# Expert rows are multiplied by their gate as they leave PSUM, and the gather adds a token's row into the token's tile

## The chip, the cores and the metric

The kernel runs on one NeuronCore of a Trainium2 chip. Its compute engines are TensorE (PE; matmuls, with the loads of their stationary operand listed apart as PEld), VectorE (DVE), ScalarE (ACT) and GpSimd (POOL); SyncE (SP) issues most of the DMA transfers. Each engine works through its own queue in order, and semaphores tie the queues together. Matmul results lie in PSUM, everything else on the core in SBUF. The metric is the time of one execution in microseconds; lower is better. Times given for the kernel are medians of several runs, while the rows of the profile come from one profiled execution.

## The reference

Three parts follow one another. Attention runs over 4 batches of 576 positions with 8 heads of 64 (pooled and banded attention, added), which gives 2304 token rows of 512 numbers. A mixture of experts updates them, and a SwiGLU layer follows. What matters here is the second part:

```python
skip_score = x @ w_skip                   # x: 2304 x 512
do_compute = skip_score > 0
xc = x[do_compute]
logits = xc @ w_gate                      # 8 experts
e_idx = np.argmax(logits, axis=1)
gate_w = softmax(logits)[np.arange(len(xc)), e_idx]
for e in range(E):
    mask = e_idx == e
    h = np.maximum(xc[mask] @ w1[e], 0.0)      # 512 -> 1024
    y[mask] = gate_w[mask, None] * (h @ w2[e]) # 1024 -> 512
out[do_compute] = xc + y
```

and the third: `g = x @ w_gate; val = x @ w_val; out = (silu(g) * val) @ w_out` with 1536 hidden units. So each token that takes part gets its expert's row times one number, its gate, and that is added to the token's own row.

## The kernel before, in words

The 2304 tokens are 18 tiles of 128 (NTILE); tile i lies in SBUF as xr[i], 128 partitions of 512 float32 numbers. Every expert has 192 slots (CAP). The kernel has three stages.

**Planned stage (0 to about 193 us).** Attention, and for groups of two or three tiles the routing: logits by TensorE, then a chain of small VectorE operations that gives every token a slot number, idx (line 796), and its gate, gw (line 805). GpSimd then scatters the tile's rows, split in two float16 halves (xhl), to their slots in a DRAM buffer xs by an indirect DMA (g_x, line 858). The order of all this is not written by hand. A class Plan takes a list of operations, each with an engine, a cost, what it needs and a priority, lists them by simulated time, and emits them in that order; where it sees TensorE waiting, it puts filler matmuls on zeros (fill, line 411). After the stage's first 14 tiles, xa (line 824) loads expert 0's rows transposed; the last 4 tiles (NOH) reach expert 0 by one-hot matmuls (line 845) instead, which write into the same PSUM banks xb, and scatter their rows a little later.

**Experts (193 to 337 us).** This order is written by hand, in a loop over e from 0 to 7. SP loads weights through six staging tiles stg (lines 361, 364), ACT and VectorE split each into two float16 halves (w, lines 340 and 343); h (hp, line 1060 for expert 0 and line 1048 for the others), yb (the last 64 slots, line 1079) and ya (the first 128, line 1084) are matmuls. The output leaves PSUM times 2^-8, a fixed scale of the split, by VectorE (y_put_short, line 1088) and ACT (y_put_long, line 340), and SP writes it to a DRAM buffer ys (lines 1091, 1097). Staging is a closed loop: a new load is issued when a conversion frees its tile. For tiles 0 to 2 the rows of the last expert come by matmuls with a selection matrix (sel_y, sel_p, lines 1117 to 1132), so that they need not pass through DRAM.

**SwiGLU (337 us to the end).** While its first gv steps run, the later tiles are fetched: GpSimd gathers each token's row from ys into a tile yg (xp_g, line 1202), and VectorE multiplies it by the token's gate and adds the token's row (xp_1, line 1210):

```python
dve.scalar_tensor_tensor(out=t if i > 2 else xr[i], in0=t, scalar=gw[:, i:i + 1],
                         in1=xr[i], op0=ALU.mult, op1=ALU.add)
```

Then the tile is split (xphl) and transposed by SP's DMA. A gather is issued three tiles ahead. Each gv step is 12 matmuls into two PSUM tiles; ACT (sg, line 1262), VectorE (sg, line 1267), ACT (u) and GpSimd (u, line 346) turn the result into the next operand. At the same time conv_next turns one half-tile after another of the SwiGLU weights into float16 pairs: ACT (lines 1156, 1157), VectorE (stg, line 1163, and cb, line 1164), ACT and GpSimd (w, line 346).

## Time and profile before

| | us |
|---|---|
| median of 3 runs | 780.03 (777.61 to 780.44) |
| the profiled execution | 783.18 |
| its span | 781.0 |
| PE busy | 731.2 (94%) |
| DVE busy | 387.4 (50%) |
| ACT busy | 337.0 (43%) |
| POOL busy | 235.1 (30%) |
| line 1210 on DVE, tiles 3 to 17 (15 adds) | 31.9 |

The busy shares are averages over three stages with different limits: DVE is at 50% over the span, though in the stretch from 345 to 465 us it has hardly a gap, and after that hardly any work. So what a change is worth is read from the stretch it touches, and each stretch is listed apart in the section of rows below.

### The profile page before, as it was taken

Reading aid. Unit: us, or ns where it says so; the run is one execution under the profiler, and the core shown is the slowest. Engines: PE = TensorE matmul, PEld = TensorE weight load, DVE = VectorE, ACT = ScalarE, POOL = GpSimd, SP = SyncE. Lnnn points to the kernel's source line nnn. Section 1 sums busy time; section 2 is a strip of 40 time slices with the busy share of each in tenths; the row PEclk is TensorE's granted clock in tenths of the full one; section 3 lists DMA queues with packets and bytes.
Section 4 is the critical chain, followed back from the end, with each engine's and each line's share of the span. In section 5 each row is a group of like instructions: output and inputs, shape, how many; then the busy total and the mean of one; then the engine's idle time right before and its main releaser. Section 6 shows DMA issues by size and latency. Waiting matters only on the chain.

```text
span 781.0 us, 16260 instructions
## 1 busy us (share of the span) xinstructions
PE 731.2 (94%) x6699; PEld 485.5 (62%) x6699; DVE 387.4 (50%) x740; ACT 337.0 (43%) x650; POOL 235.1 (30%) x217
## 2 busy tenths in 40 slices
PE   9997879899799989979998789999999999999998
PEld 6776767778688867856665444466456546655653
DVE  6684687786678877769998980011001101100110
ACT  5673555442567756737667660122112202211210
POOL 5346565444000000437667660022002201210210
PEclk9998889999999999999999999999999999999999
DMA  8889878452999999845677711100000000000001
GB/s 271 243 267 243 190 197 194 137 132 86 310 309 344 315 306 303 279 151 186 168 192 197 177 28 40 41 14 1 14 28 1 1 27 14 1 14 28 1 0 41
DMA packets 88803, 107.23 MB, mean 137 GB/s; under 512 B 44720, under 2 KB 62130, under 8 KB 88151
## 3 DMA queue, kind: packets, MB, share of 16 engines
q1 hardware_dynamic: 84791, 98.23, 44.1%
q0 software_dynamic: 2880, 6.89, 2.9%
q8 instruction: 53, 0.87, 0.5%
q10 hardware_dynamic: 1056, 1.05, 0.4%
q14 instruction: 23, 0.19, 0.1%
HBM read 81.69 MB, written 17.30 MB: 127 GB/s over the span
## 4 chain that ended last, share of the span: by engine, by line
PE 41%; DVE 11%; issue 2%; ACT 2%; POOL 1%; DVEq 0%; ACTq 0%
PE gvp L1254 23%; PE op L1284 17%; DVE yg L1210 4%; DVE stg L1163 2%; DVE cb L1164 2%; DVE sg L1267 1%; DVE xphl L346 1%; ACT stg L1156 1%; POOL w L346 0%; DVE xpT L346 0%; ACT stg L1157 0%; PE xpp L1218 0%; ACT u L340 0%; ACT xpT L340 0%; ACT sg L1262 0%
## 5 line engine op out<-in xcount | busy, mean ns | idle before, releaser
L1254 PE MATMUL gvp<-xpT,w 128*128 128x384 f16 (+1 forms) x1776 | 283.8, 322 | 7.8 <-ACT sg L1262 3.6
L1254 PEld LDWEIGHTS <-w 128*128 128x128 f16 x1776 | 170.9, 98 | 119.9 <-issue 9.8
L1267 DVE SCALAR_TENSOR_TENSOR sg<-sg,gvp 128x384 f32<-128x384 f32 x72 | 39.6, 550 | 227.2 <-PE gvp L1254 222.6
L346 POOL TENSOR_TENSOR u<-sg,u 128x384 f16<-128x384 f32 x72 | 67.3, 935 | 256.8 <-ACT u L340 256.5
L1284 PE MATMUL op<-w,u 128*128 128x512 f16 x648 | 141.0, 379 | 3.3 <-ACT sg L1262 1.8
L1284 PEld LDWEIGHTS <-u 128*128 128x128 f16 x648 | 63.4, 98 | 79.6 <-issue 4.0
L343 DVE SCALAR_TENSOR_TENSOR w<-stg,w 128x1024 f16<-128x1024 f32 x64 | 77.8, 1244 | 17.6 <-ACT w L340 17.5
L340 ACT ACTIVATE u<-sg 128x384 f16<-128x384 f32 x72 | 37.5, 521 | 109.4 <-DVE sg L1267 109.3
L346 POOL TENSOR_TENSOR w<-cb,w 128x512 f16<-128x512 f32 x36 | 49.8, 1383 | 99.1 <-ACT w L340 97.8
L340 ACT ACTIVATE w<-stg 128x1024 f16<-128x1024 f32 x64 | 65.3, 1050 | 12.5 <-DMA stg<-in_moe_w 11.6
L340 ACT ACTIVATE y<-op 128x512 f32<-128x512 f32 x18 | 10.7, 596 | 117.6 <-PE op L1284 117.6
L1048 PEld LDWEIGHTS <-w 128*128 128x128 f16 x672 | 57.1, 100 | 4.9 <-issue 3.3
L1048 PE MATMUL hp<-xe,w 128*128 128x192 f16 x672 | 58.2, 250 | 0.0
L1262 ACT ACTIVATE sg<-gvp 128x384 f32<-128x384 f32 x72 | 35.0, 486 | 38.5 <-PE gvp L1254 37.6
L1084 PE MATMUL ya<-w,hT 128*128 128x512 f16 (+1 forms) x216 | 42.9, 356 | 0.0
L1164 DVE SCALAR_TENSOR_TENSOR cb<-stg 128x512 int32<-128x512 int32 x36 | 40.9, 1135 | 3.4
L511 PE MATMUL qkd<-qks,identh 128*128 128x192 f16 x192 | 34.8, 350 | 0.0
L340 ACT ACTIVATE w<-cb 128x512 f16<-128x512 f32 x36 | 22.7, 630 | 26.8 <-DVE cb L1164 26.7
L411 PE MATMUL wbank<-wz 128*128 128x252 bf16 x209 | 31.3, 290 | 2.3 <-POOL wz L407 1.3
L1084 PEld LDWEIGHTS <-hT 128*128 128x128 f16 x216 | 20.5, 98 | 20.3 <-issue 1.6
L1210 DVE SCALAR_TENSOR_TENSOR yg<-yg,gw,x 128x512 f32<-128x512 f32 x15 | 31.9, 2135 | 0.0
L539 POOL TENSOR_TENSOR vr<-vr 72x1024 f32<-72x1024 f32 x8 | 19.0, 2372 | 39.5 <-DMA vr<-in_vr 39.5
(146 smaller groups left out, 877.5 us busy)
## 6 DMA issues: line engine op xcount, KB each, us to landing
stg<-in_moe_w SPq DMA_DIRECT2D x64, 512.0 KB
qk<-in_qk SPq DMA_DIRECT2D x24, 384.0 KB
stg<-in_moe_w_out SPq DMA_DIRECT2D x12, 512.0 KB
stg<-in_moe_w_gate SPq DMA_DIRECT2D x11, 512.0 KB
stg<-in_moe_w_val SPq DMA_DIRECT2D x11, 512.0 KB
vw<-in_vw SPq DMA_DIRECT2D x18, 284.4 KB
vr<-in_vr SPq DMA_DIRECT2D x8, 576.0 KB
up<-outd SPq DMA_DIRECT2D x18, 256.0 KB
```

Of the source, the lines that this page charges most:

```text
L340: act.activation(out=o, in_=i, func=func, scale=s)
L343: dve.scalar_tensor_tensor(out=o, in0=i, scalar=s, in1=h, op0=op, op1=ALU.subtract)
L346: eng.tensor_tensor(out=o, in0=i, in1=h, op=ALU.subtract)
L511: pe.matmul(out=p[:, n], lhsT=identh, rhs=qk_at(u, n, m // 4).rearrange("p b (g r) -> p b g r", r=4)[:, :, :, m % 4], start=(m == 0), stop ...
L1048: pe.matmul(out=p, lhsT=wt[e, kk][:, wl, m * 128:(m + 1) * 128], rhs=xe[e][:, xl + kk, :], start=(n == 0), stop=(n == 11))
L1084: pe.matmul(out=p, lhsT=hT[e][:, hl, m, 0:128], rhs=w[:, o:o + n], **f)
L1164: dve.scalar_tensor_tensor(out=b, in0=hi_w, scalar=3, in1=lo_w, op0=ALU.logical_shift_left, op1=ALU.bitwise_or)
L1210: dve.scalar_tensor_tensor(out=t if i > 2 else xr[i], in0=t, scalar=gw[:, i:i + 1], in1=xr[i], op0=ALU.mult, op1=ALU.add)
L1254: pe.matmul(out=pp[n][:, o:o + width], lhsT=w[:, wl, n, kk * 128:(kk + 1) * 128], rhs=xpT[blk][:, xl + kk, o:o + width], start=(j == 0), s ...
L1262: act.activation(out=s, in_=gs[a][0], func=AF.Silu, scale=1.0 / (XS * WS))
L1267: dve.scalar_tensor_tensor(out=s, in0=s, scalar=1.0 / XS, in1=p1, op0=ALU.mult, op1=ALU.mult)
L1284: pe.matmul(out=p, lhsT=u[:, ul, t * 128:(t + 1) * 128], rhs=w[:, wl, f % 2, :], start=(n == 0), stop=(n == 3 * NF - 1))
```

## The change

Before, a gathered row is multiplied by its gate on VectorE, after the gather, where the token is on the partition. Now the gate is applied at the expert's output, where a slot is on the partition. For that the gates have to be brought from token order to slot order:

- A DRAM buffer gwd holds one number per slot; SP writes zeros into it in the planned stage (in zero_ys).
- gate_put(i): GpSimd scatters the 128 gates of tile i to their slots by an indirect DMA of 4 bytes each. For tiles 0 to 13 it is an operation of the plan (named gy) that needs the group's gw and idx, with cost 1.05 and priority -20, against -100 for the scatter of the rows; for tiles 14 to 17 it is issued after the plan.
- gate_load: after expert 0's h, SP loads gwd as a tile gs, 128 partitions x 2 x 8, by three DMAs that wait for all 18 scatters.
- gate_scale: one VectorE operation multiplies gs by 2^-8, after expert 0's short product is issued.
- y_put_short, y_put_long and sel_y take a column of gs as their scale instead of the constant.
- xp_g gathers straight into the token's tile xr[i], with the DMA adding (compute_op=add). xp_1 and its 18 VectorE operations are gone, as is the tile yg; sel_p keeps a plain add.

```diff
+            def gate_put(i):
+                d = pool.indirect_dma_start(out=gwd[:, :], out_offset=bass.IndirectOffsetOnAxis(ap=idx[:, i:i + 1], axis=0),
+                                            in_=gw[:, i:i + 1], in_offset=None, bounds_check=OV0 - 1, oob_is_err=False)
...
+                if i < NTILE - NOH:
+                    pl.add(("gy", i), "POOL", 1.05, lambda i=i: gate_put(i), need=[("gw", gi), ("gk", gi), "zx"], late=1.9, pri=-20)
...
+            for i in range(NTILE - NOH, NTILE):
+                gate_put(i)
...
+        def gate_load():
+            v_ = gwd.rearrange("(e s) o -> s (e o)", e=E)
+            for n, (p0, s0, m) in enumerate(((0, 0, 128), (0, 128, 64), (64, 128, 64))):
+                rows_ready(sp.dma_start(out=gs_[p0:p0 + m, min(n, 1), :], in_=v_[s0:s0 + m, :]), gates)
+
+        def gate_scale():
+            dve.tensor_scalar(out=gs_, in0=gs_, scalar1=2.0 ** -8, scalar2=None, op0=ALU.mult)
...
-            dve.tensor_scalar(out=t, in0=yp.pop((e, 1)), scalar1=2.0 ** -8, scalar2=None, op0=ALU.mult)
+            dve.tensor_scalar(out=t, in0=yp.pop((e, 1)), scalar1=gs_[:, 1, e:e + 1], scalar2=None, op0=ALU.mult)
...
-            hi_(t, yp.pop((e, 0)), 2.0 ** -8)
+            hi_(t, yp.pop((e, 0)), gs_[:, 0, e:e + 1])
...
-            dve.scalar_tensor_tensor(out=xr[i], in0=p, scalar=gw[:, i:i + 1], in1=xr[i], op0=ALU.mult, op1=ALU.add)
-            xg[i] = xr[i]
+            dve.tensor_tensor(out=xr[i], in0=p, in1=xr[i], op=ALU.add)
...
-            t = t2.tile([128, DM], F32, tag="t2", name="yg")
-            pool.indirect_dma_start(out=t, out_offset=None, in_=ys[:, :],
-                                    in_offset=bass.IndirectOffsetOnAxis(ap=idx[:, i:i + 1], axis=0))
-            xg[i] = t
+            pool.indirect_dma_start(out=xr[i], out_offset=None, in_=ys[:, :],
+                                    in_offset=bass.IndirectOffsetOnAxis(ap=idx[:, i:i + 1], axis=0), compute_op=ALU.add)
+            xg[i] = xr[i]
...
-        def xp_1(i):
-            t = xg[i]
-            dve.scalar_tensor_tensor(out=t if i > 2 else xr[i], in0=t, scalar=gw[:, i:i + 1], in1=xr[i], op0=ALU.mult, op1=ALU.add)
...
             if e == 0:
                 h_first()
+                gate_load()
...
             y_short(e)
+            if e == 0:
+                gate_scale()
```

Because the plan has 14 operations more, it orders the whole stage anew: TensorE's order holds 257 fillers, where it held 209. GpSimd's order at the end of the planned stage, before (x3 means three in a row; seld is the first operation of the experts that GpSimd has):

```order
L346 TENSOR_TENSOR xhl<-x,xhl 128x512
L858 DMA xs<-xhl,idx 1536x1024 x2
L346 TENSOR_TENSOR xhl<-x,xhl 128x512 x3
L858 DMA xs<-xhl,idx 1536x1024 x3
L346 TENSOR_TENSOR xhl<-x,xhl 128x512 x2
L858 DMA xs<-xhl,idx 1536x1024 x4
L1106 MEMSET seld 128x128
```
and of the changed kernel, whose lines are one to some twenty higher (gwd<-gw is a scatter of gates):

```order
L860 DMA xs<-xhl,idx 1536x1024 x3
L347 TENSOR_TENSOR xhl<-x,xhl 128x512 x2
L868 DMA gwd<-gw,idx 1536x1
L347 TENSOR_TENSOR xhl<-x,xhl 128x512
L868 DMA gwd<-gw,idx 1536x1 x5
L860 DMA xs<-xhl,idx 1536x1024 x3
L347 TENSOR_TENSOR xhl<-x,xhl 128x512
L860 DMA xs<-xhl,idx 1536x1024 x4
L868 DMA gwd<-gw,idx 1536x1 x4
L1128 MEMSET seld 128x128
```
Six scatters of gates have come in ahead of the three scatters of rows that xa waits for, five of them directly, and four stand at the end.

SP's order at the start of the experts, before (stg is a weight load; w1 by line 361, w2 by line 364):

```order
L1037 DMA_TRANSPOSE xe<-xs 128x8x192
L361 DMA stg<-in_moe_w 128x1024 x4
L364 DMA stg<-in_moe_w 128x2x512 x4
L1091 DMA ys<-yb 64x256 x2
L361 DMA stg<-in_moe_w 128x1024 x2
```
and of the changed kernel:

```order
L1051 DMA_TRANSPOSE xe<-xs 128x8x192
L362 DMA stg<-in_moe_w 128x1024 x4
L365 DMA stg<-in_moe_w 128x2x512 x2
L1103 DMA gs<-gwd 128x8x1
L1103 DMA gs<-gwd 64x8x1 x2
L365 DMA stg<-in_moe_w 128x2x512 x2
L1113 DMA ys<-yb 64x256 x2
L362 DMA stg<-in_moe_w 128x1024 x2
```
The three loads of gates (gs<-gwd) stand behind the second of expert 1's four w2 loads, and the other two w2 loads behind them.

VectorE's order at the same place, before (hT is the split of h, w that of a weight tile):

```order
L343 SCALAR_TENSOR_TENSOR hT<-hp,hT 128x192 x4
L343 SCALAR_TENSOR_TENSOR w<-stg,w 128x1024 x2
L1088 TENSOR_SCALAR yb<-yb 128x256
L343 SCALAR_TENSOR_TENSOR w<-stg,w 128x1024 x2
L343 SCALAR_TENSOR_TENSOR hT<-hp,hT 128x192 x2
```
and of the changed kernel:

```order
L344 SCALAR_TENSOR_TENSOR hT<-hp,hT 128x192 x4
L1106 TENSOR_SCALAR gs<-gs 128x16
L344 SCALAR_TENSOR_TENSOR w<-stg,w 128x1024 x2
L1110 TENSOR_SCALAR yb<-yb,gs 128x256
L344 SCALAR_TENSOR_TENSOR w<-stg,w 128x1024 x2
```
The scaling of gs has come in ahead of the four weight conversions and yb.

VectorE's order in a pair of steps of SwiGLU's first part, before:

```order
L346 TENSOR_TENSOR xphl<-yg,xphl 128x512
L1210 SCALAR_TENSOR_TENSOR yg<-yg,gw,x 128x512
L1267 SCALAR_TENSOR_TENSOR sg<-sg,gvp 128x384
L1163 SCALAR_TENSOR_TENSOR stg<-stg 128x512
L1164 SCALAR_TENSOR_TENSOR cb<-stg 128x512
L1267 SCALAR_TENSOR_TENSOR sg<-sg,gvp 128x384
L1163 SCALAR_TENSOR_TENSOR stg<-stg 128x512
L1164 SCALAR_TENSOR_TENSOR cb<-stg 128x512
L346 TENSOR_TENSOR xphl<-yg,xphl 128x512
L1210 SCALAR_TENSOR_TENSOR yg<-yg,gw,x 128x512
```
and of the changed kernel:

```order
L347 TENSOR_TENSOR xphl<-x,xphl 128x512
L1284 SCALAR_TENSOR_TENSOR sg<-sg,gvp 128x384
L1184 SCALAR_TENSOR_TENSOR stg<-stg 128x512
L1185 SCALAR_TENSOR_TENSOR cb<-stg 128x512
L1284 SCALAR_TENSOR_TENSOR sg<-sg,gvp 128x384
L1184 SCALAR_TENSOR_TENSOR stg<-stg 128x512
L1185 SCALAR_TENSOR_TENSOR cb<-stg 128x512
L347 TENSOR_TENSOR xphl<-x,xphl 128x512
```
The add of the gathered tile, which stood between xphl and sg once in two steps, is gone; the rest keeps its order.

## Rows read from the trace of the kernel before

Of a timeline, the columns are start, duration, engine (SPq: SP's DMA issue), line, operation, out<-in and count, and in brackets the idle time before and what ended it. Of a group by line: busy time and mean ns of one, then idle time before and what ended it.

**Rows 1.** The page's chain, by line, in shares of the span
```profile
PE gvp L1254 23%; PE op L1284 17%; DVE yg L1210 4%; DVE stg L1163 2%; DVE cb L1164 2%; DVE sg L1267 1%; DVE xphl L346 1%; ACT stg L1156 1%; POOL w L346 0%; DVE xpT L346 0%; ACT stg L1157 0%; PE xpp L1218 0%; ACT u L340 0%; ACT xpT L340 0%; ACT sg L1262 0%
```

**Rows 2.** Busy by stretch: start:end, length; PE, PEld, DVE, ACT, POOL; PEclk, DMA, GB/s
```profile
193.00:337.00 144.00, 133.03 (x1379) 108.52 (x1380) 108.03 (x157) 92.47 (x154) 9.10 (x8) 0.98 0.98 302
345.00:465.00 120.00, 109.61 (x669) 64.50 (x669) 110.33 (x116) 80.37 (x155) 81.34 (x68) 1.00 0.61 163
465.00:781.00 316.00, 312.08 (x1718) 168.06 (x1717) 27.80 (x50) 59.23 (x114) 43.94 (x49) 1.00 0.05 17
```

**Rows 3.** Timeline: start, duration, engine, line, operation, out<-in; one stall of PE
```profile
425.86 7.96 PE L1254 MATMUL gvp<-xpT,w 128*128 128x384 f16 x48 [1.81 <-ACT sg L1262]
```

**Rows 4.** Groups by line: the add of a gathered tile
```profile
L1210 DVE SCALAR_TENSOR_TENSOR yg<-yg,gw,x 128x512 f32<-128x512 f32 x15 | 31.9, 2135 | 0.0
```

**Rows 5.** Timeline of two steps in the first SwiGLU part
```profile
367.17 2.92 DVE L1210 SCALAR_TENSOR_TENSOR yg<-yg,gw,x 128x512 f32<-128x512 f32 x1
368.37 1.16 POOL L346 TENSOR_TENSOR w<-cb,w 128x512 f16<-128x512 f32 x1
...
425.66 0.75 DVE L1210 SCALAR_TENSOR_TENSOR yg<-yg,gw,x 128x512 f32<-128x512 f32 x1
426.79 3.28 DVE L1163 SCALAR_TENSOR_TENSOR stg<-stg 128x512 int32<-128x512 int32 x1
```

**Rows 6.** Timeline, end of the experts
```profile
326.57 5.41 PE L1084 MATMUL ya<-w,hT 128*128 128x256 f16 x48
332.04 0.75 DVE L1210 SCALAR_TENSOR_TENSOR x<-yg,gw,x 128x512 f32<-128x512 f32 x1 [0.69 <-DMA yg<-ys,idx]
336.50 0.38 PE L1129 MATMUL selx<-sely,sel 128*128 128x256 f16 x2 [3.66 <-DVEq L1358]
```

**Rows 7.** Timeline, end of the planned stage
```profile
178.30 1.05 POOL L858 DMA_INDIRECT xs<-xhl,idx  x1 [0.30 <-issue]
182.50 0.16 DVE L805 RECIPROCAL gw<-ges 128x3 f32<-128x3 f32 x1
185.09 0.81 PE L838 MATMUL xb<-xa,identh 128*128 128x384 f16 x4 [0.94 <-DMA xa<-xs]
187.72 3.28 PE L411 MATMUL wbank<-wz 128*128 128x252 bf16 x29
192.97 0.75 PE L1060 MATMUL hp<-xe,w 128*128 128x192 f16 x7 [0.65 <-DVE xe L853]
```

**Rows 8.** Groups by line: fillers, and scatters of rows
```profile
L411 PE MATMUL wbank<-wz 128*128 128x252 bf16 x209 | 31.3, 290 | 2.3 <-POOL wz L407 1.3 <-DVE od L605 0.5 <-issue 0.4
L858 POOL DMA_INDIRECT xs<-xhl,idx x18 | 20.3, 1129 | 13.0 <-DVE idx L796 3.4 <-DVE gw L805 3.3 <-issue 2.9
```

**Rows 9.** Timeline, start of the experts
```profile
204.76 6.38 SPq L364 DMA_DIRECT2D stg<-in_moe_w  x4
207.91 1.21 DVE L343 SCALAR_TENSOR_TENSOR w<-stg,w 128x1024 f16<-128x1024 f32 x1
209.72 1.06 ACT L340 ACTIVATE w<-stg 128x1024 f16<-128x1024 f32 x1 [0.23 <-DMA stg<-in_moe_w]
210.66 0.42 DVE L1088 TENSOR_SCALAR yb<-yb 128x256 f32<-128x256 f32 x1
211.00 1.06 ACT L340 ACTIVATE w<-stg 128x1024 f16<-128x1024 f32 x1 [0.22 <-DMA stg<-in_moe_w]
214.53 2.64 PE L1048 MATMUL hp<-xe,w 128*128 128x192 f16 x30
```

**Rows 10.** Timeline, the load of the router's weights and its reader
```profile
24.98 0.50 SPq L470 DMA_DIRECT2D w9f<-in_moe_w_skip  x1
30.59 0.24 ACT L340 ACTIVATE w<-w9f 128x36 f16<-128x36 f32 x1 [0.68 <-DMA w9f<-in_moe_w_skip]
```

**Rows 11.** Timeline, 48 yb matmuls after a gap, and of a later expert
```profile
205.05 4.36 PE L1079 MATMUL yb<-w,hT 128*64 128x256 f16 x48 [3.99 <-DVE hT L343]
239.00 2.81 PE L1079 MATMUL yb<-w,hT 128*64 128x256 f16 x48
```

More of the change, by code (lines that the diff above doesn't have):

```diff
@@ L328, in body @@
     outd = dr.tile([NT // 4, DM], F32, name="outd")
+    gwd = dr.tile([OV0, 1], F32, name="gwd")
     cs = cp.tile([128, C_KEEP], F32, name="cs")
@@ L366, in w_load, with rows_ready @@
         sg[e, c] = t
-    wt, wps, scat, xe = {}, [], [], {}
-    def rows_ready(d):
-        for w in scat:
+    wt, wps, scat, gates, xe = {}, [], [], [], {}
+    def rows_ready(d, all_=scat):
+        for w in all_:
             tc.add_manual_dep(d.ins, w.name, mybir.DependencyInfo(mybir.DependencyClass.Sync, mybir.DependencyReason.DATA),
@@ L482, in zero_ys @@
                 z32 = wz.bitcast(F32)
+                sp.dma_start(out=gwd.rearrange("(p a) o -> p (a o)", p=128), in_=z32[:, 0:OV0 // 128])
                 for r in (ZROW - CAP, ZROW - CAP + 128):
@@ L863, in g_x @@
                 scat.append(d.ins)
+            def gate_put(i):
+                d = pool.indirect_dma_start(out=gwd[:, :], out_offset=bass.IndirectOffsetOnAxis(ap=idx[:, i:i + 1], axis=0),
+                                            in_=gw[:, i:i + 1], in_offset=None, bounds_check=OV0 - 1, oob_is_err=False)
+                tc.declare_no_dep(d.ins, group="gates", reason="distinct rows")
+                tc.add_to_no_dep_group("gates", d.ins)
+                gates.append(d.ins)
             pl = Plan({"bank": 7, "fb": 1, "qk": NQK, "qks": 2, "qkh": 2, "vw": NV, "vr": 1, "vd": 2, "dP": 2, "dT": 2,
@@ L1007, in body @@
         wps.append(P_("wp", 18 - NPRE))
+        gs_ = slp.tile([128, 2, E], F32, name="gs")
         over = cp.tile([128, E], F32, name="over")
@@ L1120, in sel_y @@
             y = sel[k][:, :, o:o + w]
-            hi_(y[:, 0, :], p, 2.0 ** -8)
-            lo_(y[:, 1, :], p, y[:, 0, :], 2.0 ** -8)
+            hi_(y[:, 0, :], p, gs_[:, min(k, 1), E - 1:E])
+            lo_(y[:, 1, :], p, y[:, 0, :], gs_[:, min(k, 1), E - 1:E])
         def sel_p(i):
@@ L1200, in xp_g @@
         def xp_g(i):
-            t = t2.tile([128, DM], F32, tag="t2", name="yg")
-            pool.indirect_dma_start(out=t, out_offset=None, in_=ys[:, :],
-                                    in_offset=bass.IndirectOffsetOnAxis(ap=idx[:, i:i + 1], axis=0))
-            xg[i] = t
+            pool.indirect_dma_start(out=xr[i], out_offset=None, in_=ys[:, :],
+                                    in_offset=bass.IndirectOffsetOnAxis(ap=idx[:, i:i + 1], axis=0), compute_op=ALU.add)
+            xg[i] = xr[i]
         xs_ = {}
-        def xp_1(i):
-            t = xg[i]
-            dve.scalar_tensor_tensor(out=t if i > 2 else xr[i], in0=t, scalar=gw[:, i:i + 1], in1=xr[i], op0=ALU.mult, op1=ALU.add)
-            blk, o = divmod(i, 3)
-            if o == 0 and i:
-                xpT[blk] = pools["h6"].tile([128, 8, BLK], F16, tag="h6", name="xpT")
         def xp_p(i):
@@ L1223, in xp_h @@
                 blk, o = divmod(i, 3)
+                if blk not in xpT:
+                    xpT[blk] = pools["h6"].tile([128, 8, BLK], F16, tag="h6", name="xpT")
                 hi_(xpT[blk][:, 0:4, 128 * o:128 * o + 128], xs_[i], 1.0)
@@ L1231, in xp_l @@
             blk, o = divmod(i, 3)
+            if blk not in xpT:
+                xpT[blk] = pools["h6"].tile([128, 8, BLK], F16, tag="h6", name="xpT")
             v_ = xpT[blk][:, :, 128 * o:128 * o + 128]
@@ L1330, in body @@
                 y_put_short(e)
-                for i in range(3):
-                    xp_1(i)
                 conv_next(False)
@@ L1380, in body @@
                 xp_l(i + 1)
-        xp_1(3)
         conv_next(False)
@@ L1392, in xp_next @@
                     xp_g(i + 3)
-                if i + 1 < NTILE:
-                    xp_1(i + 1)
                 nxt[0] += 1
@@ L1433, in body @@
                 xp_g(6 + n)
-                for i in ((4, 5), (), (6,))[n]:
-                    xp_1(i)
             conv_next()
```

1 line of the change is left out of this document (removed).

## The prediction, made before the changed kernel was timed

> **What bounds the kernel now.** I read the chain of waits first [rows 1]: TensorE's gv matmuls and output matmuls lead it, and the largest entry of another engine is the VectorE operation that this change deletes (line 1210, 4% of the span). Next the busy times by stretch [rows 2]. From 465 us on TensorE works 312.1 of 316.0 us, so nothing that VectorE gives up there can shorten it. From 345 to 465 us TensorE works 109.6 of 120.0 us while VectorE works 110.3: the 10.4 us of idle TensorE are all that this stretch can give back. The two earlier stretches run before any token row is gathered; the change takes nothing out of them and adds its scatters and loads there. The timeline of TensorE shows where the idle time lies: mostly after 418 us, in stalls of 1 to 2 us between whole steps, such as [rows 3].
>
> **SwiGLU's first part (removed: 15 of the 18 adds, line 1210).** The group of line 1210 says 15 x 2135 ns = 31.9 us [rows 4], but an add has no such length by itself. The row at 367.17 lasts 2.92 us and ends 0.56 us after GpSimd's w operation (368.37 + 1.16 = 369.53); the one at 425.66 takes 0.75 us, and there the next VectorE operation with both tensors in SBUF, line 1163, takes 3.28 us [rows 5]. So a VectorE operation with two inputs from SBUF is held up while GpSimd works on its tensors, and with the add gone the next one in the queue is held. The Trainium skill, SBUF — State Buffer, section "Who interferes with whom", states this as an exclusive lock on shared ports, in which the later engine is blocked fully; by that rule the 31.9 us shrink to 15 x 0.75 = 11.2 us, against 31.9 us by the group alone, and the trace agrees with the rule (2.92 here, 0.75 there). I take what the rows give: 15 x 0.75 = 11.2 us less VectorE work in this stage. That is enough to let TensorE close most of its 10.4 us, since VectorE was 92% busy (110.3 of 120.0) and is now about 83%. Bounds of the gain: 10.4 (all idle time) and 0 (the hold passes on and the same step ends as late as before). I take 9.5, near the upper end, because the stall in [rows 3] ends on a sg operation (line 1262 on ACT), and VectorE's sg (line 1267), which TensorE's tiles also wait for, stands right behind an add in VectorE's order. Late next would be TensorE itself. The three adds of line 1132 on selx stay, as plain adds.
>
> **End of the experts (removed: 3 adds).** The adds for tiles 0 to 2 stand in VectorE's queue ahead of the last expert's output, and the last one waits 0.69 us for its gather and ends at 332.79 [rows 6]. Behind it come two conversion operations, two sely operations, and the matmuls with the selection at 336.50, for which TensorE had waited 3.66 us. Without the adds that chain starts when TensorE's second half of the long product ends, 326.57 + 5.41 = 331.98 [rows 6], or up to 3 us earlier for the VectorE part: 3 x 0.75 + 0.69 = 2.9. Bounds 1 and 3; I take 2.8. The gathers of the later tiles are still issued three tiles ahead of their use; that lead, and the add that no longer follows, hide an adding transfer that is slower than a plain one by no more than such an add, 0.75 us, and probably by much more.
>
> **Planned stage (added: 18 scatters of one number per token).** A scatter of rows costs GpSimd 1.05 us and 0.30 us to the next [rows 7]; none of so few bytes is in the trace, so its bounds are 0.3 (only the issue) and the same 1.1 [rows 8]; I take the 0.98 + 0.30 = 1.28 us of its neighbours, since the issue and not the bytes is what the engine shows. 14 stand inside the planned order: 18 us of GpSimd, of which only those near the end matter. Six (tiles 8 to 13) come in the order just before the last three row scatters on which the transposed load xa waits; before, the last of those ended at 179.35 and TensorE had xa at 185.09, 0.94 us late already [rows 7]. The order of the changed kernel puts 5 of them directly ahead: 5 x 1.28 = 6.4 us, less what GpSimd idled there. The planner knows this and fills TensorE's waits: its order has 257 fillers, 209 before; at the 0.113 us that one takes in the long runs near the end (29 in 3.28 us [rows 7]; over the whole stage the mean is 0.290 [rows 8]), 48 fillers are 5.4 us. Both ways say 5 to 6; bounds 2 (fillers standing in waits that were idle anyway) and 11 (below). I take +5. The last four, after the plan, land while the first expert is under way and delay nothing.
>
> **Start of the experts (added: the load of the gates and one scaling).** SP issues three loads of 1024, 512 and 512 single numbers after the second w2 load of expert 1, in the middle of the row at 204.76 that lasts 6.38 us, so at about 207.4 [rows 9]. VectorE reaches the scaling at 207.9, where before it did a weight conversion, and in order it then holds four conversions of 1.21 us each, yb, and behind them expert 1's h. When do the gates land? ACT waits for weights that arrive one by one at 209.72 and 211.00, 1.3 us apart; two more stand ahead of the gates in the same queue, so about 211.0 + 2 x 1.3 = 213.6, and then 2048 tiny packets. The nearest row of such a load is that of the router's weights: issued by 25.48, its reader was released at 30.59, 5.1 us, behind other loads too [rows 10]. Of these 5.1 I allow 40 to 65% (2.0 to 3.4 us) for the packets, since the loads ahead are counted already: 215.6 to 217.0, and the first h matmul of expert 1 can start the scaling, four conversions and yb later, 0.2 (a VectorE operation of few elements takes 0.16, the one of 182.50 in [rows 7]) + 4 x 1.21 + 0.42 = 5.5 us: 221.1 to 222.5, against 214.53 [rows 9], 6.6 to 8.0 us later. An idle gap also costs clock: after 3.99 us without work the 48 yb matmuls took 4.36 us, and elsewhere 2.81 [rows 11], so another 1.6. The experts that follow are bound by TensorE (133.0 of 144.0 us), and nothing returns the loss. The lower bound is a landing 5.1 us after the issue without the queue, 212.5: TensorE at 218.0, +3.5; the upper one 11. I take +8.
>
> The Trainium skill, DMA: Bandwidth & Descriptors, section "Anatomy of one DMA — SWDGE (gpsimd) path", gives a small transfer about 2.0 us in all; by it the gates would be there at about 209.5, the stall would be some 1.5 us in place of 8, and the sum 6 us better. The trace speaks against it for loads in a busy queue (5.1 us), so I do not take it.
>
> **Sum.** +5 (planned stage) + 8 (start of experts) - 2.8 (their end) - 9.5 (SwiGLU's first part) = +0.7 us. The profiled execution took 783.18 us (span 781.0), the median of the runs is 780.03, 3.15 less; 783.9 - 3.15 = 780.7, say 781.
>
> **Rivals.** *Faster, the gates come early* (27%). The loads do not stand behind the weights, land after the 5.1 us of the row, cost +3.5, and the plan's fillers lie partly in old idle time, +3 to +4: 3.5 + 3.5 - 2.8 - 9.5 = -5.3, 774.7 us. For it: the three loads are small and SP issues them early. Against it: 1.3 us between weights that already fill the queue.
> *Slower, GpSimd held by the gates* (25%). GpSimd works in order, and its gate scatter now needs gw besides the slot. Before, the gw of this group was written at 182.50 [rows 7], after the row scatters had been issued. If the gates of tiles 11 to 13 hold GpSimd until then, three gates and three row scatters follow: 182.5 + 6 x 1.28 = 190.2, 10.8 us later than 179.35. That is +11 in place of +5: 787 us. It decides from a loss of 8 us in that stage. For it: nothing else changed in what gw waits for. Against it: the changed order has gw within a few VectorE rows of idx.
> *The adds were not what held TensorE* (8%). The hold by GpSimd passes to the next operation and the steps end as before; the SwiGLU part gives 0 to 2 and the sum is +8 to +10: 789 us.
> *No measurable change*, my forecast, 40%.
>
> **Chances and range.** About 0.5% of the time (776.1 to 783.9) is what a measurement can tell from no change. Faster 27% (first rival), same 40%, slower 33% (25 + 8). The range 772 to 789 reaches from the first rival with the gain at its upper bound (774.7 - 0.9 - 1.5 for fillers of no cost) to the last; the forecast's own range is 777 to 785.
>
> **What would show it.** In the changed trace: PE busy in the stretch of the first gv steps within 2 us of its length (right) or still 5 us short (wrong); VectorE's first scaling of gs waiting for a transfer, with a wait of 5 to 10 us (right), under 2 us (first rival); the first hp of the experts 4 to 6 us after 192.97 [rows 7] (right), 9 or more (second rival); the operation behind the missing add at 2 to 3 us where GpSimd works beside it. The forecast fails if the start of the experts costs under 3 us, or if the planned stage costs over 8.

## The result, and the profile after

The changed kernel took 790.75 us in the median of 4 runs (787.74 to 793.74), the kernel before 780.24 beside it (777.61 to 780.68): a ratio of 1.0142, with a 95% interval of 1.0096 to 1.0187. It is slower by 7.5 to 14.6 us, where I had forecast 781 and no measurable change, and 1.75 us outside my range.

The profiled execution after is the fastest of its four (787.74 us, span 785.9), that of before was slower than every timed run of it (783.18). So the two traces stand 4.9 us apart where the medians stand 10.5 apart. In what follows a trace shows where something waits; how much it costs is taken from the ratios of the experiments, each measured beside before on one chip.

Busy times of the changed kernel by stretch (PE, PEld, DVE, ACT, POOL; clock, DMA, GB/s), the second moved by 5 us against [rows 2]:

```profile
193.00:337.00 144.00, 131.75 (x1374) 105.91 (x1375) 105.11 (x151) 91.33 (x149) 16.66 (x15) 0.98 0.93 290
350.00:470.00 120.00, 113.30 (x724) 68.46 (x725) 107.08 (x105) 82.23 (x160) 91.23 (x71) 0.99 0.88 169
```
In the experts TensorE now works 131.8 of 144.0 us (133.0 before), and in SwiGLU's first part still only 113.3 of 120.0, though VectorE has 15 adds less: 6.7 us short, where the prediction had put under 2 for right and 5 for wrong. VectorE's busy time there fell by 3 us, not by 11 (by 5 in the stretch moved by 8.5 us, as far as the selx matmuls moved).

The end of the planned stage, answering to [rows 7]:

```profile
184.50 1.20 POOL L860 DMA_INDIRECT xs<-xhl,idx  x1 [0.31 <-issue]
187.28 0.97 POOL L860 DMA_INDIRECT xs<-xhl,idx  x1 [0.30 <-issue]
193.69 0.82 PE L840 MATMUL xb<-xa,identh 128*128 128x384 f16 x4 [0.79 <-DMA xa<-xs]
197.91 2.32 PE L1074 MATMUL hp<-xe,w 128*128 128x192 f16 x26 [0.65 <-DVE xe L855]
```
The three row scatters that xa waits for now end at 188.2 and no longer at 179.4, behind the gates. The first h matmul comes at 197.9, 4.9 us later than before.

The start of the experts, answering to [rows 9]:

```profile
210.84 5.16 SPq L1103 DMA_DIRECT2D gs<-gwd  x3
219.46 0.17 DVE L1106 TENSOR_SCALAR gs<-gs 128x16 f32<-128x16 f32 x1 [8.49 <-DMA gs<-gwd]
220.82 0.42 PE L1062 MATMUL hp<-xe,w 128*128 128x192 f16 x3 [3.75 <-DVE w L344]
224.62 1.62 PE L1062 MATMUL hp<-xe,w 128*128 128x192 f16 x9 [0.47 <-DVE w L344]
```
SP issues the loads of the gates from 210.8 to 216.0 (5.16 us for three). VectorE stands 8.49 us at the scaling, and expert 1's h, which stood in one piece at 214.53 before, comes in bits and runs from 224.62 on. So it went as the prediction had it: start of the steady h at 224.6, where I had 221.1 to 222.5 for an unshifted kernel, so 226.0 to 227.4 for one that comes 4.9 us later.

The end of the experts, answering to [rows 6]:

```profile
334.19 1.54 POOL L1222 DMA_INDIRECT x<-ys,idx  x1 [0.30 <-issue]
334.66 3.92 DVE L1184 SCALAR_TENSOR_TENSOR stg<-stg 128x512 int32<-128x512 int32 x1
335.17 2.86 POOL L347 TENSOR_TENSOR w<-cb,w 128x512 f16<-128x512 f32 x2
335.27 5.41 PE L1098 MATMUL ya<-w,hT 128*128 128x256 f16 x48
339.30 0.48 DVE L344 SCALAR_TENSOR_TENSOR sely<-yb,gs,sely 128x256 f16<-128x256 f32 x1
345.02 0.58 PE L1151 MATMUL selx<-sely,sel 128*128 128x256 f16 x2 [3.48 <-ACTq L1376]
```
TensorE waits 3.48 us before selx (3.66 before). The adds are gone from VectorE's queue, but the conversion that was behind them, line 1184, is now the one that is held, 3.92 us, beside a gather and two w operations of GpSimd; sely comes at 339.3. In this kernel none of the 2.8 us came. The selx matmuls also start slow (0.58 us for two, 0.38 before).

Two groups before, which [rows 4] does not have:

```profile
L1163 DVE SCALAR_TENSOR_TENSOR stg<-stg 128x512 int32<-128x512 int32 x36 | 29.3, 813 | 0.0
L1202 POOL DMA_INDIRECT yg<-ys,idx x18 | 21.0, 1166 | 11.9 <-DVE x L1132 8.8 <-issue 1.4 <-DVE xpT L346 0.3
```
The same two after, and TensorE's longest stall there in SwiGLU, answering to [rows 3]:

```profile
L1184 DVE SCALAR_TENSOR_TENSOR stg<-stg 128x512 int32<-128x512 int32 x36 | 58.4, 1624 | 0.0
L1222 POOL DMA_INDIRECT x<-ys,idx x18 | 31.6, 1755 | 9.2 <-DVE x L1154 6.0 <-issue 1.4 <-PE selx L1153 0.3
```
```profile
447.45 13.13 PE L1271 MATMUL gvp<-xpT,w 128*128 128x384 f16 x72 [2.88 <-ACT sg L1279]
```
The stalls of TensorE still end on sg, up to 2.88 us. What became of the adds' 31.9 us is in the group of stg, which went from 29.3 to 58.4 us, and the gathers take 1.76 us that took 1.17 before; the experiments take these apart.

### The profile page after: what moved, and what is told of

Read it like the earlier page. It is cut to its first block, busy times and chain, and to the rows that moved or that the text cites. A ratio compares the mean times of both kernels' runs of the same rounds, so it can differ in the third digit from the quotient of the medians.

```text
span 785.9 us, 16391 instructions
## 1 busy us (share of the span) xinstructions
PE 737.8 (94%) x6747; PEld 487.7 (62%) x6747; DVE 387.3 (49%) x723; ACT 337.2 (43%) x650; POOL 264.3 (34%) x235
## 3 DMA queue, kind: packets, MB, share of 16 engines
q10 hardware_dynamic: 1056, 1.05, 0.4%
## 4 chain that ended last, share of the span: by engine, by line
PE 46%; DVE 6%; issue 2%; ACT 1%; POOL 1%; DVEq 0%; ACTq 0%
PE gvp L1271 28%; PE op L1301 17%; DVE stg L1184 4%; DVE sg L1284 1%; DVE cb L1185 1%; POOL w L347 1%; DVE xphl L347 1%; POOL u L347 0%; ACT stg L1177 0%; PE xpp L1231 0%; ACT u L341 0%; PE selx L1151 0%; ACT stg L1178 0%; PE selx L1153 0%; ACT sg L1279 0%
## 5 line engine op out<-in xcount | busy, mean ns | idle before, releaser
L347 POOL TENSOR_TENSOR u<-sg,u 128x384 f16<-128x384 f32 x72 | 76.0, 1055 | 248.2 <-ACT u L341 248.1
L347 POOL TENSOR_TENSOR w<-cb,w 128x512 f16<-128x512 f32 x36 | 55.8, 1568 | 93.4 <-ACT w L341 93.4
L1062 PEld LDWEIGHTS <-w 128*128 128x128 f16 x672 | 57.1, 100 | 10.5 <-DVE w L344 7.0
L1184 DVE SCALAR_TENSOR_TENSOR stg<-stg 128x512 int32<-128x512 int32 x36 | 58.4, 1624 | 0.0
L1185 DVE SCALAR_TENSOR_TENSOR cb<-stg 128x512 int32<-128x512 int32 x36 | 39.2, 1090 | 3.8 <-DVE stg L1184 0.5
L412 PE MATMUL wbank<-wz 128*128 128x252 bf16 x257 | 37.7, 288 | 1.8 <-POOL wz L408 1.3
L1222 POOL DMA_INDIRECT x<-ys,idx x18 | 31.6, 1755 | 9.2 <-DVE x L1154 6.0
```

The lines of the kernel that those rows point to most:

```text
L347: eng.tensor_tensor(out=o, in0=i, in1=h, op=ALU.subtract)
L412: pe.matmul(out=wbank[:, 260:512], lhsT=wz[:, 0:128], rhs=wz[:, 0:252], start=True, stop=True)
L1062: pe.matmul(out=p, lhsT=wt[e, kk][:, wl, m * 128:(m + 1) * 128], rhs=xe[e][:, xl + kk, :], start=(n == 0), stop=(n == 11))
L1184: dve.scalar_tensor_tensor(out=lo_w, in0=hi_w, scalar=-0x80000000, in1=lo_w, op0=ALU.bitwise_and, op1=ALU.bitwise_or)
L1185: dve.scalar_tensor_tensor(out=b, in0=hi_w, scalar=3, in1=lo_w, op0=ALU.logical_shift_left, op1=ALU.bitwise_or)
```

## The experiments

Each ratio is to before on the same chip; 1% is 7.8 us. Where a run leaves something out of the result, its expectation says so. e1 to e4 ran on one chip, e5 to e8, e9 to e11, e12 to e15 and e16 to e18 on one each.

**e1, no gates.** What the adding gather and the missing adds bring by themselves.

```diff
-                if i < NTILE - NOH:
-                    pl.add(("gy", i), "POOL", 1.05, lambda i=i: gate_put(i), need=[("gw", gi), ("gk", gi), "zx"], late=1.9, pri=-20)
...
-                gate_load()
...
-                gate_scale()
...
-            dve.tensor_scalar(out=t, in0=yp.pop((e, 1)), scalar1=gs_[:, 1, e:e + 1], scalar2=None, op0=ALU.mult)
+            dve.tensor_scalar(out=t, in0=yp.pop((e, 1)), scalar1=2.0 ** -8, scalar2=None, op0=ALU.mult)
```
The constant comes back for ya and sely in the same way.

> The changed kernel without any gates: no scatters, no load, no scaling, and the expert rows leave PSUM times the old constant, so the multiplication by the gate is left out of the result. The gather that adds stays, the 18 adds on VectorE are gone. Planned stage and experts are then those of before (first hp at 193, scatter order as before). Theory A (the profile after: the hold by GpSimd passes on to line 1184, and an adding gather keeps GpSimd 1.8 us in place of 1.2): the part from the selx matmuls to the end gains 4 to 6 us, so 774 to 776 us. Rival (my prediction: the adds themselves held TensorE): 2.8 + 9.5 us gained, 768 us.

Measured: 777.1 us, 0.9937 (0.9913 to 0.9961), 4.9 us under before. Theory A; my 12.3 us did not come. The wait at the selx matmuls, 3.66 us before, and the group of stg in its trace:

```profile
334.22 0.38 PE L1145 MATMUL selx<-sely,sel 128*128 128x256 f16 x2 [2.28 <-DVEq L1367]
L1178 DVE SCALAR_TENSOR_TENSOR stg<-stg 128x512 int32<-128x512 int32 x36 | 59.3, 1647 | 0.0
```
So 1.4 us of the 2.8 forecast for the end of the experts come here, where no gate is applied.

**e2, gates only.** The complement: the gates as in the change, with the old gather and a plain add.

```diff
-            pool.indirect_dma_start(out=xr[i], out_offset=None, in_=ys[:, :],
-                                    in_offset=bass.IndirectOffsetOnAxis(ap=idx[:, i:i + 1], axis=0), compute_op=ALU.add)
...
+            t = t2.tile([128, DM], F32, tag="t2", name="yg")
+            pool.indirect_dma_start(out=t, out_offset=None, in_=ys[:, :],
+                                    in_offset=bass.IndirectOffsetOnAxis(ap=idx[:, i:i + 1], axis=0))
...
+            dve.tensor_tensor(out=t if i > 2 else xr[i], in0=t, in1=xr[i], op=ALU.add)
```

> The changed kernel with the plain gather of before and an add of two tensors on VectorE in the place of the old multiply-add; the gates are scattered, loaded and applied as in the change. Theory A: planned stage +4.9 and start of the experts +6, partly given back at a later wait for weights, nothing gained in SwiGLU: +8 to +14 us on before, 788 to 794 us, about the changed kernel or up to 5 above it. Rival (the loss comes from the adding gathers and GpSimd's longer hold): within 3 us of before, 778 to 783 us.

Measured: 795.9 us, 1.0171 (1.0134 to 1.0208): the gates cost 13 us, the rival is out. Its groups, with the add still there:

```profile
L1232 DVE TENSOR_TENSOR yg<-yg,x 128x512 f32<-128x512 f32 x15 | 31.8, 2123 | 0.0
L1185 DVE SCALAR_TENSOR_TENSOR stg<-stg 128x512 int32<-128x512 int32 x36 | 30.9, 857 | 0.0
```
Here the adds take 31.8 us and the conversion stg 30.9 (0.86 each). In the changed kernel the adds are gone and stg takes 58.4 (1.62 each): 27.5 of the 31.8 us went over to the next operation that wants two tensors from SBUF. Only 4.3 us of VectorE's busy time really went.

**e3, late use.** The same loads, but VectorE converts expert 1's weights before it scales the gates.

```diff
+                if e == 1 and m == 4:
+                    gate_scale()
+                    y_put_short(0)
+                    y_put_long(0, 0, DM)
...
-            if e == 0:
-                gate_scale()
...
-                y_put_short(e)
+                if e:
+                    y_put_short(e)
```

> The changed kernel, with the scaling of gs and expert 0's two outputs moved behind the fifth h step of expert 1, so that VectorE converts expert 1's weights first. The loads of the gates stay where they are. Theory A (VectorE stood 8.5 us at the scaling, and expert 1's weights behind it): the 96 h matmuls of expert 1 start about 217 instead of being spread from 216.7 to 233.5, the run gets 5 to 8 us shorter than the changed kernel, 783 to 786 us. Rival (the loads of the gates themselves slow the weights behind them in the queue): 0 to 2 us shorter, 789 to 791 us.

Measured: 784.73 us, 1.0037 (1.0009 to 1.0066), 8 us under the changed kernel. Expert 1's h in its trace:

```profile
218.25 1.13 PE L1062 MATMUL hp<-xe,w 128*128 128x192 f16 x11
220.12 7.19 PE L1062 MATMUL hp<-xe,w 128*128 128x192 f16 x85 [0.75 <-DVE w L344]
```
One gap of 0.75 us is left of the stall. The wait at the scaling was worth 8 us (4 to 12 with both intervals), as the prediction had it.

**e4, no scatter in the plan.** All 18 behind it (`for i in range(0, NTILE): gate_put(i)`).

> The changed kernel with all 18 scatters of gates behind the plan, none inside it; the planned order is that of before, 209 fillers. Theory A: first hp of the experts back at 193 (198 in the changed kernel), but 18 scatters at 1.28 us end at 215 at the earliest, the gates land at about 222 to 224 and VectorE stands until then, so the start of expert 1 is at 228 to 230 (225 in the changed kernel): 789 to 796 us, no gain. Rival (the cost in the plan came from the extra DMA writes and not from the order): first hp still 2 us or more after 193.

Measured: 800.28 us, 1.0240 (1.0201 to 1.0279), the worst of the first four. First hp at 189.5, but:

```profile
220.21 2.46 SPq L1105 DMA_DIRECT2D gs<-gwd  x3
224.64 0.17 DVE L1108 TENSOR_SCALAR gs<-gs 128x16 f32<-128x16 f32 x1 [19.98 <-DMA gs<-gwd]
```
VectorE stands 20.0 us at the scaling, since 18 scatters come one after another and SP holds the weights behind its wait for them. The rival is out, the loss was larger than expected. The same rows tell something else: no weight load had been issued for 16 us, and the gates are there 4.4 us after the first issue, where the changed kernel, with weights in the queue, needs 8.6.

**e5, the gather copies.** e1 with `compute_op=ALU.add` left out, nothing else.

> The kernel without gates of the run e1_no_gates, and here the gather copies instead of adding, so neither the gate nor the token's own row gets into the result of a gathered tile. Theory A1 (the adding form of the gather, 1.8 us on GpSimd in place of 1.2, is part of what took the gain: 10 us more of GpSimd in the stretch of the first gv steps): the part from the selx matmuls to the second block of output matmuls (126.3 us in e1_no_gates, 128.6 before) takes 122 to 124 us, the run 2 to 4 us less than e1_no_gates, 773 to 775 us. Rival (only the tensor operations of GpSimd hold VectorE): within 1 us of e1_no_gates, 776 to 778 us.

Measured: 768.49 us, 0.9849 (0.9816 to 0.9882): 6.9 us less than e1 (0.9937; 4 to 10 us with both intervals), twice what I expected. From the first selx matmul to the end of the span the traces have 444.5 us before, 442.3 in e1 and 433.1 in e5, so the gain lies in SwiGLU. The wait at selx is 1.14 us in e5. GpSimd's rows of a pair of gv steps, and the stg of VectorE that is held there, in e1 (adding), then in e5 (copying):

```profile
371.85 1.35 POOL L347 TENSOR_TENSOR w<-cb,w 128x512 f16<-128x512 f32 x1 [2.10 <-ACT w L341]
373.35 1.83 POOL L1216 DMA_INDIRECT x<-ys,idx  x1 [0.15 <-issue]
374.62 1.52 POOL L347 TENSOR_TENSOR u<-sg,u 128x384 f16<-128x384 f32 x1
374.73 3.93 DVE L1178 SCALAR_TENSOR_TENSOR stg<-stg 128x512 int32<-128x512 int32 x1
375.49 1.75 POOL L347 TENSOR_TENSOR w<-cb,w 128x512 f16<-128x512 f32 x1
376.61 1.50 POOL L347 TENSOR_TENSOR u<-sg,u 128x384 f16<-128x384 f32 x1
380.21 1.34 POOL L347 TENSOR_TENSOR w<-cb,w 128x512 f16<-128x512 f32 x1 [2.10 <-ACT w L341]
```
```profile
369.98 1.35 POOL L347 TENSOR_TENSOR w<-cb,w 128x512 f16<-128x512 f32 x1 [2.10 <-ACT w L341]
371.48 1.24 POOL L1216 DMA_INDIRECT x<-ys,idx  x1
372.74 0.93 POOL L347 TENSOR_TENSOR u<-sg,u 128x384 f16<-128x384 f32 x1
372.87 3.33 DVE L1178 SCALAR_TENSOR_TENSOR stg<-stg 128x512 int32<-128x512 int32 x1
373.61 1.17 POOL L347 TENSOR_TENSOR w<-cb,w 128x512 f16<-128x512 f32 x1
374.73 0.91 POOL L347 TENSOR_TENSOR u<-sg,u 128x384 f16<-128x384 f32 x1
377.74 1.34 POOL L347 TENSOR_TENSOR w<-cb,w 128x512 f16<-128x512 f32 x1 [2.10 <-ACT w L341]
```
GpSimd's operations start at the same distances, but behind an adding gather (1.83 against 1.24 us) each of the three next operations ends 0.59 us later (1.52, 1.75, 1.50 against 0.93, 1.17, 0.91). The next w starts 8.36 us after the first one in e1 and 7.76 in e5. That 0.59 us lies in the loop of a pair: VectorE's stg is held until about 0.55 us after the end of GpSimd's last operation, in both (378.66 behind 378.11, 376.20 behind 375.64), then come cb, ACT's w, and GpSimd's next w, which waits 2.10 us for it. 15 x 0.59 = 8.9 us, near the 6.9 measured and the 9.2 of the traces. One other difference stands beside it: in e1's trace TensorE waits once, 1.6 us, for a gather to land (xpp), in e5's never; so up to that much of the 6.9 can be the landing.

**e6, w on VectorE.** e1 with the 36 subtractions of the conversion moved off GpSimd.

```diff
-            rest_(pool, w[:, 1, n, :], bf, w[:, 0, n, :])
+            return w[:, 1, n, :], bf, w[:, 0, n, :]
...
-            if c:
-                conv_c(*c)
+            r = conv_c(*c) if c else None
...
+            if r:
+                rest_(dve, *r)
```

> The kernel without gates of the run e1_no_gates (the gate is left out of the result), and the subtraction w of the weights' conversion (36 operations, 1.59 us each) moved from GpSimd to VectorE, behind the next stg and cb. Theory A (VectorE's 31.9 us of adds went into its wait for GpSimd: the group of line 1184 went from 30.9 to 58.4 us): with half of GpSimd's tensor work gone the mean of line 1184 falls from 1.65 to under 1.1 us, VectorE takes 36 x 0.69 = 25 us more and loses about as much waiting: the run 0 to 6 us less than e1_no_gates, 771 to 777 us. Rival (VectorE is the bound by its own work): 5 to 15 us more, 782 to 792 us.

Measured: 768.23 us, 0.9850 (0.9814 to 0.9885), 6.8 us under e1. Its groups:

```profile
L347 DVE TENSOR_TENSOR w<-cb,w 128x512 f16<-128x512 f32 x36 | 33.5, 930 | 0.0
L1178 DVE SCALAR_TENSOR_TENSOR stg<-stg 128x512 int32<-128x512 int32 x36 | 25.8, 717 | 0.0
```
VectorE does 33.5 us more and waits so much less that stg falls from 1.65 to 0.72 us: with this operation gone from GpSimd it is no longer held. The wait at selx falls too, to 0.84 us (2.28 in e1). The rival is out.

**e7, e12, e13, e15: what the plan's order costs.** e7 and e13 are e3 with the 14 operations kept in the plan and nothing issued for them (`lambda i=i: None`; the last four scatters, the loads and the scaling stay); e12 lets GpSimd write zeros instead; e15 is e1 in that order; e14 is e3 again.

> The kernel of the run e3_late_use with the plan's 14 operations for the gates kept, with their cost and place, but nothing issued for them: the gates of tiles 0 to 13 stay zero in the result. The order of everything else and the 257 fillers are those of the changed kernel. Theory B (the plan's order costs the time: fillers and waits are written into the order): first hp of the experts at 197 to 200, as with the scatters. Rival (GpSimd's 18 us of scatters cost it): first hp at 190 to 195, as before, and the run 4 to 6 us shorter than e3_late_use.

> The kernel of the run e3_late_use; in the place of each of the plan's 14 scatters GpSimd reads one column of gw and writes zeros to a scratch tile twice (about 1.2 us of GpSimd, no packets); the gates of tiles 0 to 13 stay zero in the result. Order and 257 fillers as in the changed kernel. Theory D (GpSimd's time in its in-order queue is the cost): the chain as with the scatters, xa matmuls at 193 to 196, first hp at 197 to 200, time within 2 us of e14_late_use_again. Rival (the packets of 4 bytes are the cost): first hp at 190 to 194, 3 to 6 us less.

> The kernel of e7_priced_only once more, beside the others on one chip: the plan's order with nothing issued for the gates of tiles 0 to 13. Theory D: first hp 190 to 195 again, 3 to 6 us less than e14_late_use_again. Theory B (the order is the cost): the same time as e14_late_use_again within 2 us, and the first hp of this trace near that of e15_order_alone.

> The kernel of e3_late_use once more, as the measure for the other three: first hp 197 to 200, 0.1 to 0.7% over before.

> The kernel of e1_no_gates (no gates at all, the gate left out of the result) in the plan's order of the changed kernel, with its 257 fillers: nothing but the order differs from e1_no_gates, which took 0.9937 of before. Theory B (the order costs the time): 0.997 to 1.003 of before, 4 to 7 us more than e1_no_gates. Theory D (only the issued scatters cost it): 0.991 to 0.996 of before.

Measured: e7 783.04 us, 1.0028 (1.0001 to 1.0055), first hp at 192.5. Neither side came whole: the first hp is the rival's, but the time is that of e3 within 1 us by the ratios, not 4 to 6 less. So issuing the plan's 14 scatters adds little to what is left in e7 (the two intervals allow up to 4 us; e3 ran on another chip).

e12 793.02, 1.0133; e13 793.76, 1.0144; e14 807.82, 1.0349; e15 788.73, 1.0091 (1.0055 to 1.0127). The same kernels are 11 and 23 us slower on this chip than on the others (e13 and e7, e14 and e3), and before is not (780.59). First hp came at 206 to 221, and none of the four runs came as expected. e14 is far over its range (1.001 to 1.007). e12 and e13 are 14 to 15 us under e14, where their theories had within 2 us or 3 to 6 us. e15 is over both of its ranges (1.003 at most). Within e14, TensorE stood inside 48 small matmuls with nothing recorded that it waited for:

```profile
146.10 0.34 PE L633 MATMUL sl<-qks 64*64 64x70 f16 x4 [1.12 <-issue]
```
In the whole planned stage such gaps at that line sum to 10.2 us in e14, 5.5 in e15, 4.4 in e13, 2.2 in e12. So theory D and theory B could not be told apart here: e12 and e13 agree within 1 us, which speaks against GpSimd's time as the cost, but the disturbance on this chip is larger than what was asked.

**e8, hold.** The gates' whole way put where nothing should wait: scatters behind the plan, outputs of experts 0 and 1 kept unscaled, gates loaded and applied in expert 2.

```diff
+                if e == 2 and m == 1:
+                    gate_load()
+                if e == 2 and m == 5:
+                    gate_scale()
+                if e == 2 and m in (6, 7):
+                    y_put_short(m - 6)      # the rows kept, times gs
+                    y_put_long(m - 6, 0, DM)
```

> The whole change with the gates off every wait: no scatter in the plan (all 18 behind it), the outputs of experts 0 and 1 are kept unscaled in SBUF, the gates are loaded and scaled in expert 2, and the kept rows are then multiplied and stored. Theory A: planned stage as before (first hp 189 to 196), start of the experts as before, 4 more small operations on idle time, and the gain of e1_no_gates stays: 776 to 779 us, 0.6% under before. Rival (the scatters, the loads of single numbers or the late stores cost something wherever they stand): 781 to 787 us.

Measured: 796.82 us, 1.0210 (1.0175 to 1.0245), 18 us over theory A's range and 10 over the rival's. Rows of its start:

```profile
219.01 0.50 PE L1064 MATMUL hp<-xe,w 128*128 128x192 f16 x2 [2.83 <-ACT w L341]
221.46 2.00 ACT L341 ACTIVATE w<-stg 128x1024 f16<-128x1024 f32 x2 [2.51 <-DMA stg<-in_moe_w]
...
255.23 0.17 DVE L1108 TENSOR_SCALAR gs<-gs 128x16 f32<-128x16 f32 x1 [3.95 <-DMA gs<-gwd]
```
While GpSimd scatters (until 222.5), expert 1's weights come late (ACT waits 2.51 us for a load, TensorE 2.83 for ACT), and the scaling still waits 3.95 us for its loads. Theory A fell: the gates' way costs here too, where it meets the weight loads, and more than the rival had. Which of its parts costs it, the run does not take apart.

**e9, gates behind the rows.** e3, with the gates of tiles 8 to 13 needing the row scatters of tiles 11 to 13 (`need=[...] + [("gx", n) for n in (11, 12, 13)]`).

> The kernel of the run e3_late_use, with the gates of tiles 8 to 13 allowed in the plan only after the row scatters of tiles 11 to 13: the same 18 scatters, five of them now directly behind those three and not ahead (260 fillers). Theory C (GpSimd works in order, and five gates ahead of the rows that xa waits for cost 5 x 1.28 us): the xa matmuls come back from 193.7 to 185 to 189, first hp at 191 to 196, the run 3 to 6 us less than e3_late_use, 779 to 782 us. Rival (the scatters cost it by their packets, wherever in the plan): first hp at 197 to 200, within 2 us of e3_late_use.

Measured: 788.51 us, 1.0088 (1.0058 to 1.0118), worse than e3, with the first hp at:

```profile
207.71 2.48 PE L1074 MATMUL hp<-xe,w 128*128 128x192 f16 x28 [0.65 <-DVE xe L855]
```
Theory C fell as I had put it; but the plan also moved the last group's work behind the gates (its one-hot matmuls at 205.6), and a third chip was used, so the run does not isolate the five scatters.

**e10 and e11, w on VectorE with the whole change, and with the kernel before.** The edit of e6 on e9, and on the kernel before.

> The kernel of e9_gates_behind with the subtraction w of the weights' conversion on VectorE in place of GpSimd. From e6_w_on_dve against e1_no_gates (7 us less) and theory C: 771 to 776 us, the whole change with its gates then 0.7 to 1.3% under before. Rival (with the gates in, the experts' end or the later start shifts the bound back): 778 us or more.

> The kernel before, unchanged but for the subtraction w of the weights' conversion, which goes from GpSimd to VectorE: no gates, the plain gather, and the 18 multiply-adds stay on VectorE. Theory A (what costs is VectorE's wait for GpSimd, 28 us in the groups of lines 1163 and 1210 together, and not VectorE's own work): with half of GpSimd's tensor work gone the wait shrinks by more than the 25 us of new work adds to the loop, 771 to 777 us, faster than before without any gate. Rival (the adds and w together fill VectorE: 18 x 0.75 + 36 x 0.93 + the rest): 782 us or more.

Measured: e10 780.84 us, 0.9984 (0.9960 to 1.0007), no gain over before; the rival. e11 766.14 us, 0.9815 (0.9783 to 0.9848), the fastest of all, with the whole result and without any gate traffic. The stretch from 345 us of e11, then its groups:

```profile
345.00:465.00 120.00, 120.00 (x706) 68.97 (x705) 100.98 (x143) 81.03 (x155) 43.29 (x36) 1.00 0.62 158
```
```profile
L1163 DVE SCALAR_TENSOR_TENSOR stg<-stg 128x512 int32<-128x512 int32 x36 | 24.7, 687 | 0.0
L1211 DVE SCALAR_TENSOR_TENSOR yg<-yg,gw,x 128x512 f32<-128x512 f32 x15 | 14.3, 961 | 0.0
```
TensorE works 120.0 of 120.0 us. VectorE's adds, unchanged in number, fall from 2.14 to 0.96 us each.

**e16, e17, e18: the order and the scatters on one chip.** e1, e15 and e3 again.

> The kernel of e1_no_gates once more (no gates, the plan's order of before), as the measure for the next two on the same chip: 0.992 to 0.996 of before, first hp 189 to 196.

> The kernel of e15_order_alone once more, on the chip of e16. Theory B (the order written by the plan costs time wherever it runs): 4 to 12 us more than e16_no_gates_again, the idle time of the 48 sl matmuls with no releaser in the profile again 2 us or more. Rival (the order is neutral, and the stall of 5 us before those matmuls belonged to that one chip): within 2 us of e16.

> The kernel of e3_late_use for the third time, on the chip of e16 and e17. If the scatters cost time beside the order: 3 to 10 us over e17 (14 us of the time on the chip of e14 and e15 were 807.8 - 788.7 = 19). Rival (only the order counts): within 2 us of e17.

Measured: e16 776.48 us, 0.9938 (0.9911 to 0.9966); e17 774.82 (772.97 to 787.25), 0.9898 (0.9862 to 0.9934); e18 784.64, 1.0042 (1.0013 to 1.0072). Order alone is neutral here, so e15's loss belonged to that chip; scattering, loading and applying the gates costs 9.8 us (e18 against e17, medians). Rows of e17, then of e18:

```profile
181.36 0.97 POOL L859 DMA_INDIRECT xs<-xhl,idx  x1 [0.30 <-issue]
195.02 0.81 PE L839 MATMUL xb<-xa,identh 128*128 128x384 f16 x4
199.23 8.09 PE L1070 MATMUL hp<-xe,w 128*128 128x192 f16 x96 [0.65 <-DVE xe L854]
```
```profile
190.21 0.97 POOL L860 DMA_INDIRECT xs<-xhl,idx  x1 [0.30 <-issue]
196.72 0.82 PE L840 MATMUL xb<-xa,identh 128*128 128x384 f16 x4 [0.67 <-DMA xa<-xs]
200.95 8.09 PE L1074 MATMUL hp<-xe,w 128*128 128x192 f16 x96 [0.65 <-DVE xe L855]
```
The last row scatter for xa is 8.9 us later with the gates issued, the xa matmuls and the first hp only 1.7 us: in the changed order TensorE has other work and fillers there. From there to expert 1's ya the trace of e18 loses 3.6 us more, and 1.6 at the experts' end. That is 6.9 us up to selx, and the traces end 4.8 apart. The profiled execution of e17 took 780.77 us, 6 us over its median, so these rows can understate what the scatters cost the planned stage.

## Why the prediction was wrong

My sum was -12.3 for the removal and +5 and +8 for the gates. In ratios (x 7.8 us per cent) the removal brought -4.9 (e1, e16), and the gates cost +13 where they stand alone (e2). That makes +8.5, and the changed kernel is +11 (7.5 to 14.6). So the price of the gates was about right and the gain was not. The gates' cost has two parts: VectorE's wait at the scaling, +8 (1.0142 against 1.0040), and the rest, +8 (e3 and e18 against e1 and e16: 1.0 point). These two and -4.9 make +11 by construction; against the 13 of e2 they are 3 us too much, within the intervals.

- **Start of the experts, +8: right,** in mechanism and size (e3). The landing behind the weights was the point: 219.5, 8.6 us after the first issue, against 4.4 in e4, where no weights were in the queue. It was not the 2 us that the Trainium skill (DMA: Bandwidth & Descriptors, "Anatomy of one DMA — SWDGE (gpsimd) path") gives for DMAs that GpSimd issues, while these go out from SP; and the first rival falls with it. Part of the delay the prediction did not have: SP needed 5.16 us to issue the three loads (2.46 in e4).
- **SwiGLU's first part, -9.5, and the end of the experts, -2.8: wrong, and here the forecast fails.** That the adds were worth about 12 us is true: e5, without them and with a copying gather, is 11.8 us under before. The step that failed is the sentence that the lead of three tiles and the missing add "hide an adding transfer". I looked at when the transfer lands, and there it is hidden nearly (the median landing went from 5.1 to 7.8 us; no wait of TensorE for it in the changed kernel, one of 1.6 us in e1). But the adding form also keeps GpSimd 0.59 us longer per gather, and GpSimd's work holds VectorE's next conversion, in a loop that sets the pace of the step; the prediction had this term at nothing. That took back 6.9 us. The end of the experts follows the same hold: of the 3.66 us at selx 1.14 are left with a copying gather (e5), 2.28 with an adding one (e1), and with w off GpSimd 0.84 (e6) and, gates included, 0.98 (e10). With the gates and w on GpSimd it is 2.8 to 3.8 us (the changed kernel, e2, e3, e7, e9, e18); why the gates add there, no run takes apart.
- **The hold that passes on: right, and no loss by itself.** I had stg at 2 to 3 us where GpSimd works beside it; held, it takes 3.05 to 4.34. 27.5 of the 31.8 us of adds moved to line 1184. But in e5 it is held too (51.6 us in all) and the 11.8 us come nevertheless: what counts is how long GpSimd's burst is, not which operation waits for it. So the third rival (8%), whose 789 us were nearest in time, had the outcome (SwiGLU gives 2.2 us in e1's trace) but not the cause, for with a copying gather the hold passes on too and SwiGLU gives 11.4.
- **Planned stage, +5: the first hp agrees, the price and its place stay open.** It came 4.9 us late, inside my 4 to 6, but traces of the unchanged order differ by 6.7 us among themselves, so one trace can't confirm it, and the match may be luck. GpSimd's delay was 8.9 us and not my 6.4 (the last row scatter for xa, 188.25 against 179.35). The order with its fillers is neutral (e17), and e7, which issues none of the plan's 14 scatters, takes as long as e3. If e7 and e3 can be compared across their two chips, most of the +8 without VectorE's wait comes with the last four scatters, the loads and the scaled outputs. In single traces the experts, from the first hp to selx, take 140.6 to 144.0 us there (e3, e7, e18) and 137.1 to 138.9 without gates (e1, e16, e17). How much is packets and how much SP's queue isn't settled.
- **Not foreseen:** that the time of the planned stage scatters. First hp came between 189.5 and 196.2 in traces of one order, and for the changed order at 192.5 to 201.0 on some chips and at 206 to 221 on one. The second rival had GpSimd's row scatters nearly right (10.8 us late, 8.9 measured), but its 11 us at TensorE did not come; e12 and e18 don't support it either.
